# Second feed-forward block of a fused attention kernel: the hi/lo split of a pair of middle blocks is issued behind the next pair's Relu and sums, and the second product begins with six of eight pairs

## The chip, the cores and the metric

One core of a Trainium2 chip runs the whole program. The metric is the time of one execution on the device in microseconds (us), the median of several runs. Beside it there is one profiled execution, whose trace gives the start and the length of nearly every instruction on the core's engines: TensorE (PE; its weight loads are listed as PEld), VectorE (DVE), ScalarE (ACT), GpSimd (POOL) and SyncE (SP), which issues most DMAs.

## The reference

The input passes through causal-by-blocks attention (4 batches, 8 heads, 576 positions, 64 wide), a feed-forward block with layer norm, and a second feed-forward block behind a two-dimensional Fourier transform. All is float32. The change lies in the last two lines of the second block:

```python
def _moe2_ref(x, w_ch1, w_ch2):            # x: (4, 576, 512)
    X = np.fft.fft(x, axis=1)
    X = np.fft.fft(X, axis=2)
    mixed = np.real(X).astype(np.float32)
    u = x + mixed
    mu = np.mean(u, axis=-1, keepdims=True)
    var = np.mean((u - mu) ** 2, axis=-1, keepdims=True)
    un = (u - mu) / np.sqrt(var + 1e-06)
    ch = np.maximum(un @ w_ch1, 0.0) @ w_ch2   # 512 -> 2048 -> 512
    return (u + ch).astype(np.float32)
```

## The kernel before

**Tiles and chunks.** The 2304 tokens are handled in nine chunks of 256, named E0 to E3, F0 to F3 and L; a chunk's rows lie in a tile X as two halves of 128 tokens. float32 products are made of float16 ones: each operand is split into a high and a low half, hi = float16(x) and lo = float16(x - hi), and three of the four products hi x hi, hi x lo and lo x hi are added up in PSUM. So each block of a product is three matmuls.

**The second feed-forward block.** E0 and F0 go through it in the plain way. The other seven chunks, in the order E1, F1, E2, F2, E3, F3, L, use a Strassen-like scheme (seven block products in place of eight) for the second product, and the change is in these.

- *First product* (`s_gemm1`, called for i = 0 to 7). Unit i makes two blocks of the middle layer, i and i + 8 ("a pair"), each from 12 matmuls with 256 columns, into one PSUM bank `g`. Five such banks go round. The weights are tiles `wq`, the layer-normed tokens the tile `xnT`, of which there is one.
- *Evacuation* (`s_out`, once for each pair). Two Relus on ScalarE (L693) write the four 128 x 128 sub-blocks of the pair into a float32 tile `hr` (four of them go round). Four sums and differences on VectorE (L701) add the Strassen combinations, so that there are seven operands of 128 x 128. ScalarE then copies all seven to float16, the hi half (L702), and VectorE subtracts to get the lo half (L703), both into a tile `hs`; one `hs` tile holds two pairs, so a chunk has hs0, hs2, hs4 and hs6.
- *Second product* (`s_gemm2_steps`, eight steps). Step function `mm(p, hb, nm, i0, i1)` adds up, in the PSUM tile `s` of product p, operand hb of pairs i0 to i1 - 1 against the prepared weights T[nm] (names beginning with tB or tT): three matmuls a pair, 24 for a whole product, 168 for the seven. Three banks go round for `s`. `got(p)` adds a finished product into X on VectorE (L726, L732, with one copy to `su` on ScalarE, L738), and `put` sends a half of X to the output.
- *Layer norm of the next chunk* stands between these steps in four parts (`ln_steps`): VectorE normalizes into `xn` (L563), ScalarE makes the hi half in `xs` (L571), VectorE the lo half (L577), and a DMA on SP's queue transposes `xs` into `xnT` (L578). There is one `xs` and one `xnT`, so each half waits for the transpose before it, and the first transpose waits until the first product of the present chunk has read `xnT`.

**What sets the order.** `ffn_items` lists the work of the chunks, the first product's eight units and then the second product's eight steps, and `merge` interleaves it with other streams by the weights that stand beside each item (2.62 for a unit; 2.3, 2.3, 0.6 and 2.6 for the steps). The framework then puts each engine's instructions in order by the place in the program less a priority: `prio(f, n)` moves what f issues ahead by n places. `s_out` has S7P = 20. Each engine runs its own list in order; engines wait for each other by semaphores.

Of the kernel before, what the change touches and what calls it, by code (L numbers as in the profile page):

```python
# [12 lines left out]
AF = mybir.ActivationFunctionType  # L13
ALU = mybir.AluOpType
# [66 lines left out]
RK = (3, 4, 0, 1, 2, 5, 5.5)  # L81
PLAIN2 = (("E", 0), ("F", 0))
YP = 60
S7P = 20
R_T = 1.0
BLOCKS = ("B11", "B21", "B22", "T1", "T3", "T2", "T4")

# [2 lines left out]
def fused_kernel(ctx: ExitStack, tc: tile.TileContext, io: dict):  # L90
    nc = tc.nc
# [13 lines left out]
    def g_tile(shape, name):  # L105


        pool = psg
        if "x" in psn:
            pool = psn["x"] if psn["n"] % (GB + GX) >= GB else psg  # L110
            psn["n"] += 1
        return pool.tile(shape, F32, tag="g", name=name)

    def d_tile(name):
        return psn["d"].tile([128, 512], F32, tag="s", name=name)
# [394 lines left out]
    def w1(ffn, k, hl, m):  # L510
        o = 512 * k + 128 * (m % 4)
        return W[ffn, 1, m // 4][:, hl, o:o + 128]
# [5 lines left out]
    hT = {}  # L518
# [151 lines left out]
    def s_gemm1(c, i):  # L670

        if i % 2 == 0:
            t = wpool.tile([128, 2, 2, 7, 128], F16, tag="w", bufs=9, name=f"hs{i}")
            hT[2, c] = hT.get((2, c), []) + [t]
        xt = xnT[2, c]
        ps = g_tile([128, 2, 256], "g1")
        for q in range(2):
            n = 0
            for k in range(KT):
                for wh, xh in ((0, 0), (0, 1), (1, 0)):  # L680
                    nc.tensor.matmul(  # L681
                        out=ps[:, q, :], lhsT=w1(2, k, wh, i + 8 * q), rhs=xt[:, xh, k, :],
                        start=(n == 0), stop=(n == 3 * KT - 1),
                    )
                    n += 1
        prio(s_out, S7P)(ps, hT[2, c][i // 2][:, i % 2], i // 4)

    def s_out(ps, h, j):

        r = fpool.tile([128, 8, 128], F32, tag="hT", bufs=4, name="hr")  # L690
        rf = r.rearrange("p b t -> p (b t)")
        for q in range(2):
            nc.scalar.activation(  # L693
                out=rf[:, 256 * q:256 * q + 256], in_=ps[:, q, :], func=AF.Relu,
                scale=W["tk"][:, j + 2 * q:j + 2 * q + 1],
            )
        for o, a, b, op in (
            (4, 0, 2, ALU.add), (6, 1, 0, ALU.subtract), (5, 4, 1, ALU.subtract),
            (7, 3, 5, ALU.subtract),
        ):  # L700
            nc.vector.tensor_tensor(out=r[:, o], in0=r[:, a], in1=r[:, b], op=op)  # L701
        nc.scalar.activation(out=h[:, 0], in_=r[:, 1:8], func=AF.Copy)  # L702
        nc.vector.tensor_tensor(out=h[:, 1], in0=r[:, 1:8], in1=h[:, 0], op=ALU.subtract)  # L703

    def s_gemm2_steps(c):

        st = {}
        x = X[c]

        inv = W["tk"][:, 6:7]  # L710

        def mm(p, hb, nm, i0=0, i1=8):
            if i0 == 0:
                st[p] = d_tile("s2")
            ps = st[p][:, 0:256]
            for i in range(i0, i1):
                h = hT[2, c][i // 2][:, i % 2]
                for hh, wh in ((0, 0), (0, 1), (1, 0)):
                    nc.tensor.matmul(  # L719
                        out=ps, lhsT=h[:, hh, hb], rhs=T[nm][:, wh, i],  # L720
                        start=(i == 0 and hh == 0 and wh == 0), stop=(i == 7 and hh == 1),
                    )

        def x_add(t, d, p=None):
            o = x[:, t, 256 * d:256 * d + 256]
            nc.vector.scalar_tensor_tensor(  # L726
                out=o, in0=st["u"] if p is None else st[p][:, 0:256], scalar=inv, in1=o,
                op0=ALU.mult, op1=ALU.add,
            )

        def u_add(p):
            nc.vector.tensor_tensor(out=st["u"], in0=st["u"], in1=st[p][:, 0:256], op=ALU.add)  # L732

        @(lambda f: prio(f, YP))
        def got(p):
            if p == 1:
                st["u"] = wpool.tile([128, 256], F32, tag="w", bufs=9, name="su")
                nc.scalar.activation(out=st["u"], in_=st[1][:, 0:256], func=AF.Copy)  # L738
                x_add(1, 0, 1)
            elif p == 2:  # L740
                x_add(1, 0, 2)
            elif p == 6:
                u_add(6)
                x_add(0, 0)
            elif p == 5:
                u_add(5)
                x_add(1, 1)
                x_add(0, 1)
            elif p == 7:
                x_add(0, 1, 7)  # L750
                x_add(0, 0, 7)
            elif p == 3:
                x_add(1, 1, 3)
            else:
                x_add(0, 0, 4)

        def put(t):
            nc.sync.dma_start(out=io["out"][slot_of[c] + t], in_=x[:, t, :])

        A11, A22, A12, S1, S2, S3, S4 = range(7)  # L760
        return [
            (2.3, lambda: mm(1, A11, "B11", 0, 7)),
            (2.3, lambda: mm(2, A12, "B21", 0, 7)),
            (0.6, lambda: (
                mm(1, A11, "B11", 7, 8), got(1), mm(2, A12, "B21", 7, 8), got(2),
            )),
            (2.6, lambda: (mm(6, S2, "T2"), got(6))),
            (2.6, lambda: (mm(5, S1, "T1"), got(5))),
            (2.6, lambda: (mm(7, S3, "T3"), got(7))),
            (2.6, lambda: (mm(3, S4, "B22"), got(3), put(1))),  # L770
            (2.6, lambda: (mm(4, A22, "T4"), got(4), put(0))),
        ]
# [5 lines left out]
    def prio(f, n=None):  # L778
        def g(*a):
            if (n or AP) <= 0:  # L780
                return f(*a)
            with tc.high_priority(n or AP):
                return f(*a)
        return g
# [638 lines left out]
    if True:  # L1423
# [40 lines left out]
        def ffn_items(ffn, order, both=(), mixed=None):  # L1464
            seq = []
            for n, c in enumerate(order):
                x = ("X", ffn, c) if ffn == 2 else ("X1", c)
                lns = [(0.0, f, (x,), None) for _, f in ln_steps(ffn, c)]
                g1_needs = ()
                if ffn == 1 and n < LNA:  # L1470
                    LN.extend(
                        (w, prio(f, LNQ), need, ("LN", c) if i == 3 else None)
                        for i, (w, f, need, _) in enumerate(lns)
                    )
                    lns = []
                    g1_needs = (("LN", c),)
                g1 = [
                    (2.62, lambda mp=mp, c=c: gemm1(ffn, c, mp), (("W", ffn, 1, mp // 2),) + g1_needs,
                     ("G1", ffn, c, mp)) for mp in range(8)
                ]  # L1480
                if ffn == 2 and c not in PLAIN2:
                    g1 = [(2.62, lambda i=i, c=c: s_gemm1(c, i), (("W", 2, 1, 3),), None) for i in range(8)]
                    g2 = [
                        (w, lambda c=c, n=n: s_steps(c)[n][1](), (("W", 2, "T"),), None)
                        for n, w in enumerate((2.3, 2.3, 0.6, 2.6, 2.6, 2.6, 2.6, 2.6))
                    ]
                elif c in both or c == mixed:
                    g2 = [
                        (5.2, lambda q=q, c=c: gemm2_both(ffn, c, q), (("W", ffn, 2, q),),
                         ("F", ffn, c, q)) for q in range(4)  # L1490
                    ]
                else:
                    g2 = [
                        (2.59, lambda t=t, q=q, c=c: gemm2(ffn, c, t, q), (("W", ffn, 2, 3),),
                         ("F", ffn, c, q) if t == 1 else None) for t in range(2) for q in range(4)
                    ]
                if c == mixed:
                    g2 = sum(([g1[2 * q], g1[2 * q + 1], g2[q]] for q in range(4)), [])
                    g1 = []
                seq.append((lns, g1, g2))  # L1500
            out = []
            prev = []
            for n, (lns, g1, g2) in enumerate(seq):
                if ffn == 1 and n == 1:
                    out += lns + g1 + prev
                    prev = g2
                    continue
                k = len(prev) - 4
                out += prev[:k]
                for i in range(4):  # L1510
                    out += (prev[k + i:k + i + 1] if prev else []) + lns[i:i + 1]
                out += g1
                prev = g2
            return out + prev
# [150 lines left out]
```

## Time and profile before

| | before |
|---|---|
| median of 3 runs | 1037.1 us (1036.9 to 1037.69) |
| profiled execution, own time | 1038.49 us |
| its span, first to last instruction | 1036.6 us |
| mean granted clock of TensorE | 0.96 |
| PE busy | 930.3 us (90%) |
| PEld busy | 692.9 us (67%) |
| DVE busy | 739.8 us (71%) |
| ACT busy | 578.6 us (56%) |
| POOL busy | 82.8 us (8%) |

The span is what the trace shows; the execution's own time is what the runs are measured by, and it holds the span and the little around it. Matmuls are pipelined, so that one that is shown as 0.27 us long may follow the one before it after 0.11 us: the rate is read from the starts. The granted clock is 1.00 at TensorE's higher level and 0.50 at its lower one; a mean between them says how a stretch was divided.

### The profile page before, as it was taken

The numbers are of one execution on the slowest core, as the hardware profiler recorded it, in microseconds if no ns is written. First come the engines' busy times: TensorE is split into PE (matmuls) and PEld (weight loads), VectorE is DVE, ScalarE is ACT, GpSimd is POOL, SyncE is SP. The second block draws the span as 40 slices with busy tenths as digits, with TensorE's granted clock in tenths as the row PEclk, the third lists the DMA queues.
The fourth block names the chain that finished last, engine by engine and source line by source line (L and its number), as shares of the span: only waits on it lengthen the run. The fifth ranks groups of instructions, "written<-read, shape, count | busy, mean of one in ns | idle before, by whom it ended". The sixth has DMA issues, their size and how long they took to land.

```text
span 1036.6 us, 19852 instructions
## 1 busy us (share of the span) xinstructions
PE 930.3 (90%) x7730; PEld 692.9 (67%) x7730; DVE 739.8 (71%) x1821; ACT 578.6 (56%) x1017; POOL 82.8 (8%) x217
## 2 busy tenths in 40 slices
PE   5576879998889989999998989999989999999997
PEld 4464744575565674768574847685867878778786
DVE  5799898676867776675488988959856565464543
ACT  5698865777676776546366765526425243252331
POOL 2100101002002010040011011100000000000000
PEclk9688989999999999999998989999999999999999
DMA  7895834667648577454134467612010110101100
GB/s 219 233 265 146 246 74 128 127 126 158 139 100 170 116 148 131 83 175 163 21 117 115 135 187 272 228 62 71 15 39 12 31 22 22 41 12 32 22 21 22
DMA packets 173022, 115.13 MB, mean 111 GB/s; under 512 B 146957, under 2 KB 155158, under 8 KB 170880
## 3 DMA queue, kind: packets, MB, share of 16 engines
q1 hardware_dynamic: 170608, 109.60, 40.9%
q0 software_dynamic: 2320, 4.25, 1.6%
q8 instruction: 61, 1.00, 0.4%
q14 instruction: 33, 0.27, 0.1%
HBM read 64.15 MB, written 11.01 MB: 73 GB/s over the span
## 4 chain that ended last, share of the span: by engine, by line
PE 28%; DVE 20%; ACT 7%; DMA 2%; issue 2%; POOL 0%; ACTq 0%; DVEq 0%; POOLq 0%
PE s L719 11%; PE g L610 6%; DVE hs L703 5%; ACT hs L702 5%; PE g L635 5%; DVE hr L701 5%; PE g L662 2%; DMA wr<-in_w 2%; PE g L681 2%; DVE tT L444 1%; DVE hT L620 1%; DVE wt L440 1%; DVE ws L220 1%; DVE ws L217 1%; ACT wr L238 1%
## 5 line engine op out<-in xcount | busy, mean ns | idle before, releaser
L610 PEld LDWEIGHTS <-wq 128*128 128x128 f16 x2112 | 206.1, 99 | 50.3 <-ACT wq L330 8.5
L635 PE MATMUL g<-wq,hT 128*128 128x512 f16 x768 | 185.9, 381 | 0.0
L719 PEld LDWEIGHTS <-hs 128*128 128x128 f16 x1176 | 117.8, 101 | 39.4 <-ACT hs L702 13.2
L681 PEld LDWEIGHTS <-wq 128*128 128x128 f16 x1344 | 131.5, 98 | 15.4
L851 PE MATMUL pv<-vh,PT 128*128 128x65 f16 (+1 forms) x800 | 104.7, 202 | 31.0 <-DMA PT<-P 27.0
L635 PEld LDWEIGHTS <-hT 128*128 128x128 f16 x768 | 74.4, 98 | 85.1 <-issue 7.1
L851 PEld LDWEIGHTS <-PT 128*128 128x128 f16 x1200 | 83.2, 100 | 55.3 <-DMA PT<-P 29.4
L703 DVE TENSOR_TENSOR hs<-hr,hs 128x896 f16<-128x896 f32 x56 | 61.1, 1092 | 57.8 <-ACT hs L702 57.8
L702 ACT ACTIVATE hs<-hr 128x896 f16<-128x896 f32 x56 | 53.2, 950 | 80.1 <-DVE hr L701 74.9
L1063 PE MATMUL st<-k,qz 128*128 128x512 f16 (+2 forms) x288 | 79.6, 330 | 15.9 <-ACT e L1085 15.9
L693 ACT ACTIVATE hr<-g,tk 128x256 f32<-128x256 f32 x112 | 46.1, 462 | 80.9 <-PE g L681 80.9
L1085 ACT ACTIVATE e<-st,aq,acf 128x384 f32<-128x384 f32 (+2 forms) x80 | 56.8, 741 | 58.9 <-DVE aq L1080 54.9
L876 DVE SCALAR_TENSOR_TENSOR P<-e,P 128x768 f16<-128x768 f32 (+2 forms) x64 | 61.9, 970 | 38.2 <-ACT P L875 38.0
L719 PE MATMUL s<-tB,hs 128*128 128x256 f16 x504 | 68.6, 296 | 17.6 <-ACT hs L702 11.1
L719 PE MATMUL s<-tT,hs 128*128 128x256 f16 x672 | 75.8, 273 | 0.0
L620 DVE SCALAR_TENSOR_TENSOR hT<-g,hT 128x512 f16<-128x512 f32 x88 | 59.8, 683 | 18.3 <-ACT hT L619 18.1
L701 DVE TENSOR_TENSOR hr<-hr 128x128 f32<-128x128 f32 x224 | 56.6, 287 | 18.6 <-ACT hr L693 15.8
L851 PE MATMUL pv<-vl,PT 128*128 128x64 f16 (+1 forms) x400 | 65.3, 202 | 0.9 <-DVE vl L864 0.8
L662 PE MATMUL g<-wq,hT 128*128 128x512 f16 x288 | 65.5, 385 | 0.3 <-DVE wq L338 0.3
L619 ACT ACTIVATE hT<-g 128x512 f16<-128x512 f32 x88 | 51.4, 588 | 24.2 <-PE g L610 23.8
L875 ACT ACTIVATE P<-e 128x768 f16<-128x768 f32 (+2 forms) x64 | 54.8, 862 | 5.3 <-DMA PT<-P 4.0
L200 ACT ACTIVATE ws<-wr 128x512 f32<-128x512 f32 (+1 forms) x48 | 39.4, 831 | 24.0 <-DMA wr<-in_w 21.1
(416 smaller groups left out, 1654.9 us busy)
## 6 DMA issues: line engine op xcount, KB each, us to landing
wr<-in_w SPq DMA_DIRECT2D x16, 1024.0 KB, 5.9
wr<-in_w SPq DMA_DIRECT2D x32, 512.0 KB, 3.9
rawv<-in_vt SPq DMA_DIRECT2D x16, 320.0 KB, 3.6
rawqk<-in_kt SPq DMA_DIRECT2D x16, 288.0 KB, 2.8
d<-ws SPq DMA_DIRECT2D x4, 1024.0 KB, 5.5
ws<-d SPq DMA_DIRECT2D x4, 1024.0 KB, 8.6
wt<-d SPq DMA_DIRECT2D x4, 1024.0 KB, 6.2
rawqk<-in_qt SPq DMA_DIRECT2D x32, 80.0 KB, 3.3
```

Of the source, the lines that this page charges most:

```text
L610: nc.tensor.matmul(out=ps[:, i, :], lhsT=w1(ffn, k, wh, m), rhs=xt[:, xh, k, :], start=(n == 0), stop=(n == 3 * KT - 1),)
L620: nc.vector.scalar_tensor_tensor(out=h[:, :, 1, :], in0=ps, scalar=0.0, in1=h[:, :, 0, :], op0=ALU.max, op1=ALU.subtract,)
L635: nc.tensor.matmul(out=ps, lhsT=h[f // 4][:, f % 4, hh, t * 128:(t + 1) * 128], rhs=w2(ffn, f, wh), start=(f == 0 and hh == 0 and wh == 0) ...
L662: nc.tensor.matmul(out=g2["b"][t], lhsT=h[f // 4][:, f % 4, hh, t * 128:(t + 1) * 128], rhs=w2(ffn, f, wh), start=(f == 0 and hh == 0 and ...
L681: nc.tensor.matmul(out=ps[:, q, :], lhsT=w1(2, k, wh, i + 8 * q), rhs=xt[:, xh, k, :], start=(n == 0), stop=(n == 3 * KT - 1),)
L701: nc.vector.tensor_tensor(out=r[:, o], in0=r[:, a], in1=r[:, b], op=op)
L702: nc.scalar.activation(out=h[:, 0], in_=r[:, 1:8], func=AF.Copy)
L703: nc.vector.tensor_tensor(out=h[:, 1], in0=r[:, 1:8], in1=h[:, 0], op=ALU.subtract)
L719: nc.tensor.matmul(out=ps, lhsT=h[:, hh, hb], rhs=T[nm][:, wh, i], start=(i == 0 and hh == 0 and wh == 0), stop=(i == 7 and hh == 1),)
L851: nc.tensor.matmul(out=out[..., 0:w], lhsT=l, rhs=v[..., 0:w], start=(n == 0), stop=(n == len(mm) - 1))
L876: nc.vector.scalar_tensor_tensor(out=P[:, 1, 0:n], in0=e, scalar=PSC, in1=P[:, 0, 0:n], op0=ALU.mult, op1=ALU.subtract)
L1063: nc.tensor.matmul(out=st[:, h, 0:n] if j < 4 else sf[:, o:o + n], lhsT=qz[:, a, q:q + 128], rhs=k[:, c, o:o + n], start=(i == 0), stop=(j ...
```

## The change

In `s_out`, the hi copy and the lo subtraction of a pair are no longer issued with it. They are kept as a function `finish` in `s_lo`, and the call for the next pair issues them, behind that pair's second Relu on ScalarE and behind its last sum on VectorE (`tc.issue_after` holds an instruction of the same engine behind the one that is named). With the eighth pair, its own two are issued as well. The priority S7P becomes 400. In the second product, the two first sums begin with pairs 0 to 5 in place of 0 to 6, and the third step does pair 6 and then pair 7 of both. The weights of these steps in `merge` change with it.

```diff
-S7P = 20
+S7P = 400
...
-        prio(s_out, S7P)(ps, hT[2, c][i // 2][:, i % 2], i // 4)
+        late_lo = s_lo.pop("f", None)
+        prio(s_out, S7P)(ps, hT[2, c][i // 2][:, i % 2], i // 4, late_lo)
+        if i == 7:
+            prio(s_lo.pop("f"), S7P)()
...
-            nc.scalar.activation(
+            got = nc.scalar.activation(
...
-            nc.vector.tensor_tensor(out=r[:, o], in0=r[:, a], in1=r[:, b], op=op)
-        nc.scalar.activation(out=h[:, 0], in_=r[:, 1:8], func=AF.Copy)
-        nc.vector.tensor_tensor(out=h[:, 1], in0=r[:, 1:8], in1=h[:, 0], op=ALU.subtract)
+            done = nc.vector.tensor_tensor(out=r[:, o], in0=r[:, a], in1=r[:, b], op=op)
+        if late_lo is not None:
+            with tc.issue_after(got.ins), tc.issue_after(done.ins):
+                late_lo()
+
+        def finish():
+            nc.scalar.activation(out=h[:, 0], in_=r[:, 1:8], func=AF.Copy)
+            nc.vector.tensor_tensor(out=h[:, 1], in0=r[:, 1:8], in1=h[:, 0], op=ALU.subtract)
+
+        s_lo["f"] = finish
...
-            (2.3, lambda: mm(1, A11, "B11", 0, 7)),
-            (2.3, lambda: mm(2, A12, "B21", 0, 7)),
-            (0.6, lambda: (
+            (2.0, lambda: mm(1, A11, "B11", 0, 6)),
+            (2.0, lambda: mm(2, A12, "B21", 0, 6)),
+            (1.3, lambda: (
+                mm(1, A11, "B11", 6, 7), mm(2, A12, "B21", 6, 7),
                 mm(1, A11, "B11", 7, 8), got(1), mm(2, A12, "B21", 7, 8), got(2),
             )),
```

On ScalarE, at the end of the first product of chunk F1 (pairs 5, 6 and 7; `hr` are the Relus' output, `hs` the split operands, `xs` the next chunk's layer norm), this stood before:

```order
L693 ACTIVATE hr<-g_9694,tk 128x256 x2
L702 ACTIVATE hs_9659<-hr 128x896
L693 ACTIVATE hr<-g_9729,tk 128x256 x2
L702 ACTIVATE hs_9728<-hr 128x896
L693 ACTIVATE hr<-g_9763,tk 128x256 x2
L702 ACTIVATE hs_9728<-hr 128x896
L571 ACTIVATE xs<-xn 128x512
```

And this stands there in the changed program:

```order
L698 ACTIVATE hr<-g_9692,tk 128x256 x2
L712 ACTIVATE hs_9657<-hr 128x896
L698 ACTIVATE hr<-g_9727,tk 128x256 x2
L712 ACTIVATE hs_9657<-hr 128x896
L698 ACTIVATE hr<-g_9761,tk 128x256 x2
L712 ACTIVATE hs_9726<-hr 128x896 x2
L571 ACTIVATE xs<-xn 128x512
```

The copy behind each pair of Relus is now that of the pair before (the tile whose number ends in 57 is hs4, pairs 4 and 5; the one in 26 is hs6), and behind the last Relus the copies of pairs 6 and 7 stand together.

On VectorE, at the same place, this stood before:

```order
L701 TENSOR_TENSOR hr<-hr 128x128 x4
L703 TENSOR_TENSOR hs_9659<-hr,hs_9659 128x896
L701 TENSOR_TENSOR hr<-hr 128x128 x4
L703 TENSOR_TENSOR hs_9728<-hr,hs_9728 128x896
L701 TENSOR_TENSOR hr<-hr 128x128 x4
L703 TENSOR_TENSOR hs_9728<-hr,hs_9728 128x896
L577 TENSOR_TENSOR xs<-xn,xs 128x512
```

And this stands there in the changed program:

```order
L706 TENSOR_TENSOR hr<-hr 128x128 x4
L713 TENSOR_TENSOR hs_9657<-hr,hs_9657 128x896
L706 TENSOR_TENSOR hr<-hr 128x128 x4
L713 TENSOR_TENSOR hs_9657<-hr,hs_9657 128x896
L706 TENSOR_TENSOR hr<-hr 128x128 x4
L713 TENSOR_TENSOR hs_9726<-hr,hs_9726 128x896 x2
L577 TENSOR_TENSOR xs<-xn,xs 128x512
```

The four sums of a pair now stand ahead of the subtraction of the pair before; at the chunk's start the sums of pairs 0 and 1 follow each other, and at its end two subtractions do.

## Rows read from the trace of the kernel before

**Rows 1.** Span and mean granted clock of the core.

```profile
core 0: 1036.6 us, clock 0.960
```

**Rows 2.** TensorE in order of time: start, length, operation, count, [idle before <- releaser].

```profile
728.78 21.12 PE L681 MATMUL g<-xnT2('E', 1)_8972,wq 128*128 128x256 f16 x192
...
774.57 21.12 PE L681 MATMUL g<-xnT2('F', 1)_9427,wq 128*128 128x256 f16 x192
795.53 2.13 PE L719 MATMUL s<-tB,hs 128*128 128x256 f16 x18
799.02 0.39 PE L719 MATMUL s<-tB,hs 128*128 128x256 f16 x2 [1.37 <-ACT hs L702]
800.15 4.90 PE L719 MATMUL s<-tB,hs 128*128 128x256 f16 x28 [0.73 <-DVE hs L703]
...
817.98 21.12 PE L681 MATMUL g<-xnT2('E', 2)_9925,wq 128*128 128x256 f16 x192
...
843.57 2.79 PE L719 MATMUL s<-tB,hs 128*128 128x256 f16 x24 [0.73 <-DVE hs L703]
846.66 0.61 PE L719 MATMUL s<-tB,hs 128*128 128x256 f16 x4 [0.30 <-DVE hs L703]
...
860.21 21.12 PE L681 MATMUL g<-xnT2('F', 2)_10423,wq 128*128 128x256 f16 x192
...
1030.06 2.78 PE L719 MATMUL s<-tT,hs 128*128 128x256 f16 x24
```

**Rows 3.** ScalarE, VectorE and SP's queue in chunk F1, in order of time.

```profile
777.39 0.84 ACT L693 ACTIVATE hr<-g,tk 128x256 f32<-128x256 f32 x2 [14.82 <-PE g L681]
777.90 1.31 DVE L701 TENSOR_TENSOR hr<-hr 128x128 f32<-128x128 f32 x4 [2.64 <-ACT hr L693]
779.30 0.95 ACT L702 ACTIVATE hs<-hr 128x896 f16<-128x896 f32 x1 [1.07 <-DVE hr L701]
...
795.77 9.29 SPq L578 DMA_TRANSPOSE xnT2('E', 2)_9925<-xs  x2
...
798.02 0.95 ACT L702 ACTIVATE hs<-hr 128x896 f16<-128x896 f32 x1 [1.42 <-DVE hr L701]
798.88 0.82 ACT L693 ACTIVATE hr<-g,tk 128x256 f32<-128x256 f32 x2
799.00 1.09 DVE L703 TENSOR_TENSOR hs<-hr,hs 128x896 f16<-128x896 f32 x1 [1.07 <-ACT hs L702]
...
800.01 1.02 DVE L701 TENSOR_TENSOR hr<-hr 128x128 f32<-128x128 f32 x4
...
801.12 0.95 ACT L702 ACTIVATE hs<-hr 128x896 f16<-128x896 f32 x1 [1.42 <-DVE hr L701]
...
802.10 1.09 DVE L703 TENSOR_TENSOR hs<-hr,hs 128x896 f16<-128x896 f32 x1 [1.07 <-ACT hs L702]
803.11 0.68 DVE L577 TENSOR_TENSOR xs<-xn,xs 128x512 f16<-128x512 f32 x1
...
805.17 1.07 DVE L726 SCALAR_TENSOR_TENSOR XxF<-s,tk,XxF 128x256 f32<-128x256 f32 x2 [0.80 <-ACT su L738]
806.97 0.63 ACT L571 ACTIVATE xs<-xn 128x512 f16<-128x512 f32 x1 [1.83 <-DMA xnT2('E', 2)_9925<-xs]
```

**Rows 4.** The same view in chunk E1: its first hi copy on ScalarE.

```profile
736.18 0.95 ACT L702 ACTIVATE hs<-hr 128x896 f16<-128x896 f32 x1 [3.73 <-DVE ln2('F', 2)_10404 L538]
```

**Rows 5.** TensorE's waits from 728 us on: waiter, releaser, sum, times, longest.

```profile
PE s L719 <- ACT hs L702: 11.1, 8, 1.7
PE s L719 <- DVE hs L703: 6.5, 10, 0.7
```

**Rows 6.** Busy time by stretch: engines' busy us (instructions), then PEclk, DMA share, GB/s.

```profile
420.00:540.00 120.00, 120.00 (x954) 85.41 (x953) 78.50 (x189) 59.00 (x110) 16.17 (x32) 1.00 0.42 116
...
800.15:817.90 17.75, 17.75 (x148) 15.29 (x149) 11.34 (x35) 2.48 (x4) 0.00 (x0) 0.90 0.12 31
...
843.57:860.20 16.63, 16.32 (x148) 14.40 (x149) 10.20 (x33) 2.48 (x4) 0.00 (x0) 1.00 0.17 33
```

More of the change, by code (lines that the diff above doesn't have):

```diff
@@ L685, in s_gemm1, with s_out @@
                     n += 1
-        prio(s_out, S7P)(ps, hT[2, c][i // 2][:, i % 2], i // 4)
-    def s_out(ps, h, j):
+        late_lo = s_lo.pop("f", None)
+        prio(s_out, S7P)(ps, hT[2, c][i // 2][:, i % 2], i // 4, late_lo)
+        if i == 7:
+            prio(s_lo.pop("f"), S7P)()
+    s_lo = {}
+    def s_out(ps, h, j, late_lo):
         r = fpool.tile([128, 8, 128], F32, tag="hT", bufs=4, name="hr")
@@ L1484, in ffn_items @@
                         (w, lambda c=c, n=n: s_steps(c)[n][1](), (("W", 2, "T"),), None)
-                        for n, w in enumerate((2.3, 2.3, 0.6, 2.6, 2.6, 2.6, 2.6, 2.6))
+                        for n, w in enumerate((2.0, 2.0, 1.3, 2.6, 2.6, 2.6, 2.6, 2.6))
                     ]
```

## The prediction

> **What bounds the kernel now.** I read four views in this order. First the span and the median of the runs: 1036.6 us from the first to the last instruction [rows 1], and 1038.49 us as that execution's own time, so 1.89 us lie around the span. The unprofiled runs have their median at 1037.1 us, 1.4 us below the profiled one; my sum is made against the profiled span and its difference is then taken from the median.
>
> Second, TensorE in order of time over the last third [rows 2]. Seven chunks (E1, F1, E2, F2, E3, F3, L) go through the changed code from 728.78 us on. Each has 192 matmuls of the first product (eight units of 24) and 168 of the second, all with 256 columns. The first product of F1 runs from 774.57 to 795.53 us: 20.96 us / 192 = 0.1092 us a matmul, 2.62 us a unit. The second product has the same rate where nothing is waited for: 124 matmuls from 846.66 to 860.21 us, 0.1093 each. So a chunk without a wait would take 360 x 0.1092 = 39.3 us. F1 takes 817.98 - 774.57 = 43.41 us and E2 takes 860.21 - 817.98 = 42.23 us. All seven run from 728.78 to the last group's 1030.06 + 24 x 0.1092 = 1032.68 us: 303.9 us, where 7 x 39.3 = 275.1 us would do. **28.8 us** are lost.
>
> Where they are lost is seen in F1 [rows 2]. After 18 matmuls of the second product (795.53 + 1.96 = 797.49) TensorE waits 1.53 us, does two at 799.02, waits again until 800.15, 0.91 us, and then needs 17.83 us for 148 matmuls that take 16.16 at the full rate: 1.67 us more. 1.53 + 0.91 + 1.67 = 4.11 us, the whole of 43.41 - 39.30. The last term is the clock: its mean is 0.90 between 800.15 and 817.90 us, so part of the stretch was granted the lower of its two levels, 1.2 instead of 2.4 GHz, after the idle time before it; E2's stretch from 843.57 on has 1.00 [rows 6]. E2 pays 0.47 us of waiting for pair 7 instead (24 matmuls from 843.57 end at 846.19, the next begins at 846.66). The waits are put down to the hi copy on ScalarE (11.1 us in all) and the lo subtraction on VectorE (6.5 us) [rows 5], 17.6 us together; the rest of the 28.8 is the clock and what the modelled ends of matmuls hide.
>
> Third, ScalarE and VectorE in F1 [rows 3], with G0 to G7 for the ends of the eight units (774.57 + 2.62 each; G7 = 795.53). The first pair shows the bare latencies: Relus from G0 + 0.20 (777.39) for 0.84 us, sums from 777.90 for 1.31 us (G0 + 2.02), hi copy at 779.30 (0.09 later). Later pairs are a loop through both engines: hi copy of pair 6 at 798.02, of pair 7 at 801.12, 3.10 us a pair. It closes as 0.95 (copy) + 0.03 + 1.01 (lo subtraction at 799.00 to the next sums at 800.01) + 1.02 (sums) + 0.09, because on VectorE the sums of a pair stand behind the subtraction of the pair before, and that waits for ScalarE's copy. TensorE gives a pair in 2.62 us, so the loop falls 0.48 us behind at each. The last subtraction ends at 803.19, G7 + 7.66.
>
> **The change part by part.** *The order of the split.* No instruction is added or taken away: eight pairs of Relus, eight times four sums, eight copies, eight subtractions per chunk, each with its old duration. On ScalarE the copy of pair i-1 now stands behind the Relus of pair i, on VectorE its subtraction behind the sums of pair i. No engine's next step then depends on the other's last one: a pair costs ScalarE 0.82 + 0.95 = 1.77 us and VectorE about 1.02 + 1.09 = 2.11 us, both under 2.62 us [rows 3], so TensorE sets the pace and the lag does not grow. With the bare latencies: Relus of pair i end at Gi + 1.04, its sums at Gi + 2.02; the copy of pair i-1 runs from Gi + 1.06 to Gi + 2.01; its subtraction from Gi + 2.04 to Gi + 3.13, that is 0.51 us after the next unit's end, where the next sums want VectorE only at + 0.71.
>
> The new wait is the copy's: it could go at G(i-1) + 2.11 and goes at Gi + 1.06, 1.57 us later, since the Relus ahead of it wait for TensorE's unit i. Behind it stand the subtraction of the same pair and the Relus of pair i+1, which come 0.8 us after the copy's end. Nothing else is behind it until the eighth pair. At the end the order is Relus 7, copy 6, copy 7; sums 7, subtraction 6, subtraction 7: subtraction 6 ends at G7 + 3.13, copy 7 at + 3.06, subtraction 7 at about + 4.2 (before: G7 + 7.66).
>
> *Six of eight pairs.* The second product now does 18 matmuls on pairs 0 to 5 of the first sum and 18 on those of the second: 36 x 0.1092 = 3.93 us that need nothing newer than pair 5, whose subtraction ends at G6 + 3.13 = G7 + 0.51. Pair 6 is wanted at G7 + 3.93 (its lo two matmuls later, + 4.15), pair 7 at + 4.58 (lo + 4.80). Against + 3.13 and + 4.2, with about 0.1 us for the hop to TensorE, 0.9 and 0.5 us are left. So no wait remains, and without idle time I expect no lower clock: the clock was at 1.00 for 120 us from 420 to 540 us with TensorE busy throughout [rows 6].
>
> *What could come late next.* The layer norm of the following chunk stands behind copy 7 and subtraction 7. Its second half needs the tile xs, held by a DMA transpose that is queued on SP and goes out when the first product is through (795.77, G7 + 0.24). A subtraction into xs at 803.11 (0.68 us) let the next use of xs begin at 806.97 [rows 3], 3.2 us from its end, so the first transpose frees xs at about G7 + 3.2, just when copy 7 ends, and the second one lands at about G7 + 8.1 to 8.5. The next first product begins at G7 + 18.3: 10 us of cover. The first sum's evacuation (additions of 1.07 us at 805.17) would end at about G7 + 6.6; its PSUM bank is wanted by the fourth group at G7 + 18.3 - 4 x 2.62 = + 7.9. Both cost nothing, and without cover every us of lateness would be one per chunk.
>
> *E1.* It begins late: VectorE still builds weight sums and a layer norm, and its first copy starts at 736.18 [rows 4], against G0 + 2.11 = 733.51, 2.7 us late. At 2.1 us a pair against 2.62 it gains 0.5 us a pair back and is even after five or six of the seven that follow. I take nothing for it; if it gained nothing, 2.7 us less the 0.5 in hand would stay, 2.2 us once.
>
> **Sum.** 7 x 39.3 in place of 303.9: -28.8 us. Span 1036.6 - 28.8 = 1007.8; profiled time 1009.7; median 1037.1 - 28.8 = **1008.3 us**. That is also nearly the bound from below, since nothing ahead of 728 us and nothing behind the last matmul is touched.
>
> **The rivals.** *Small waits remain.* My margins of 0.5 to 0.9 us come from one chunk's rows. If the hops of the new order cost 1 us more, TensorE would wait 0.5 us per chunk: 3.5 us, 1012. Against it: the latencies I use are those of a pair that found both engines idle.
> *Small waits remain and the clock still falls.* F1 lost 1.67 us to the lower level behind waits of 2.44 us, E2 nothing behind the same two waits, so a wait can cost more than itself. With 0.5 + 1.67 us in each of seven chunks: 15.2 us less gain, 1024. The Trainium skill has this as a rule: "TensorE: Matmul & The Clock Gate", section "A second HAM failure mode: psum-queue depth-cycling", says that frequent short idle times between groups of matmuls make the clock go back and forth between its levels and that throughput suffers; F1's 0.90 agrees, E2's 1.00 does not.
> *The split is not what is waited for in time*, because the copies are held longer than I think: if subtraction 7 still ended at G7 + 7.7, TensorE would wait the old 2.9 us or so and only the clock could change: 303.9 - 7 x 42.2 = 8.5 us at most, 1029 to 1037.
> *Slower: the queues go in lock step.* If in the new order every pair had to go through Relus, sums, copy and subtraction one after the other, a pair would take 0.84 + 1.31 + 0.95 + 1.09 = 4.2 us; subtraction 7 would end 7 x (4.2 - 2.62) = 11 us later than in my sum, TensorE would wait 10.5 us per chunk against 4.1 now, and the time would be 1037.1 + 7 x 6.4 = 1082. It decides from about 3.3 us a pair on, where 7 x (3.3 - 2.62) - 0.6 equals 4.1. Against it: in the new order each copy waits only for sums that were done a pair earlier.
>
> **How the numbers follow.** My forecast 0.80; small waits 0.08; with the clock 0.06; split too late 0.03; slower 0.03. A measurement of this kernel tells about 0.2%, 2 us, from no change. All but the last two cases are faster by far, so faster 0.95, same 0.02, slower 0.03. The range goes from 1006, as an unprofiled run may lose more to the clock than the profiled one did (E2's and F1's periods differ by 1.2 us), to 1016, half of the way to the third case; 0.12 are left out above.
>
> **What would show it.** After: seven chunks of about 39.3 us in TensorE's timeline, the second product's 168 matmuls in 18.3 us with no wait for hs; mean clock 1.00 from 728 us on; copies 2.62 us apart in place of 3.10; the last subtraction at about 4.2 us after the first product's end in place of 7.7. I am wrong if copies stand more than 2.7 us apart, if the wait moves to xs or xnT, or if the clock falls without an idle TensorE.

## The result, and the profile after

| | before | after |
|---|---|---|
| median | 1037.39 us (4 runs, 1036.9 to 1040.38) | 1011.16 us (4 runs, 1007.94 to 1014.2) |
| ratio, 95% interval | | 0.9741 (0.9704 to 0.9778) |
| profiled execution, own time | 1038.49 us | 1009.95 us |
| its span | 1036.6 us | 1008.2 us |
| mean granted clock | 0.96 | 0.966 |

The change makes the kernel 2.6% faster. The forecast for the profiled execution was a span of 1007.8 and a time of 1009.7 us; the median is 2.9 us above the forecast of 1008.3, and the first experiment shows where such a difference can come from.

TensorE in order of time in the changed kernel (start, length, operation, count, [idle before]), the rows that answer to [rows 2]:

```profile
729.14 21.12 PE L681 MATMUL g<-xnT2('E', 1)_8972,wq 128*128 128x256 f16 x192
...
768.44 21.12 PE L681 MATMUL g<-xnT2('F', 1)_9427,wq 128*128 128x256 f16 x192
789.40 5.40 PE L731 MATMUL s<-tB,hs 128*128 128x256 f16 x48
794.64 8.02 PE L731 MATMUL s<-tT,hs 128*128 128x256 f16 x72
...
807.74 21.12 PE L681 MATMUL g<-xnT2('E', 2)_9925,wq 128*128 128x256 f16 x192
...
964.94 21.12 PE L681 MATMUL g<-xnT2L,wq 128*128 128x256 f16 x192
...
1001.62 2.78 PE L731 MATMUL s<-tT,hs 128*128 128x256 f16 x24
```

No row of the second product, in any of the seven chunks, has an idle time in front of it. E1 takes 768.44 - 729.14 = 39.30 us, F1 39.30 too, and six chunks 964.94 - 729.14 = 235.8 us, 39.30 each. From 729.14 to 1001.62 + 2.62 = 1004.24 us the seven take 275.1 us where they took 303.9: 28.8 us less, the whole forecast gain.

The busy time by stretch over these seven chunks, first in the kernel before, then in the changed one (us; PE, PEld, DVE, ACT and POOL busy; granted clock, DMA share, GB/s):

```profile
728.80:1032.70 303.90, 286.31 (x2521) 249.13 (x2519) 173.91 (x445) 105.39 (x188) 0.00 (x0) 0.97 0.09 24
```

```profile
729.20:1004.20 275.00, 275.00 (x2521) 246.41 (x2519) 182.06 (x445) 106.29 (x188) 0.00 (x0) 1.00 0.10 26
```

The same 2521 matmuls (the seven chunks' 2520 and the last one before them); TensorE is busy throughout, and its clock is at the higher level throughout, 2.4 GHz, where it had a mean of 0.97.

ScalarE, VectorE and SP's queue in F1 of the changed kernel, which answer to [rows 3]; G7, the end of its first product, is 789.40 us:

```profile
786.98 0.84 ACT L698 ACTIVATE hr<-g,tk 128x256 f32<-128x256 f32 x2 [0.94 <-PE g L681]
787.49 1.31 DVE L706 TENSOR_TENSOR hr<-hr 128x128 f32<-128x128 f32 x4 [0.31 <-ACT hr L698]
787.71 0.95 ACT L712 ACTIVATE hs<-hr 128x896 f16<-128x896 f32 x1
788.71 1.08 DVE L713 TENSOR_TENSOR hs<-hr,hs 128x896 f16<-128x896 f32 x1
...
789.64 5.81 SPq L578 DMA_TRANSPOSE xnT2('E', 2)_9925<-xs  x2
...
790.33 0.95 ACT L712 ACTIVATE hs<-hr 128x896 f16<-128x896 f32 x1
791.34 2.25 DVE L713 TENSOR_TENSOR hs<-hr,hs 128x896 f16<-128x896 f32 x2
791.51 0.95 ACT L712 ACTIVATE hs<-hr 128x896 f16<-128x896 f32 x1 [0.23 <-DVE hr L706]
792.72 0.63 ACT L571 ACTIVATE xs<-xn 128x512 f16<-128x512 f32 x1 [0.25 <-DMA xnT2('E', 2)_9925<-xs]
...
797.36 0.63 ACT L571 ACTIVATE xs<-xn 128x512 f16<-128x512 f32 x1 [2.46 <-DMA xnT2('E', 2)_9925<-xs]
```

The copies of pairs 5 and 6 start at 787.71 and 790.33, 2.62 us apart in place of 3.10. Relus wait for TensorE (0.94 us a pair) and the sums for the Relus (0.31): both engines have room now, and TensorE sets the pace. The last subtraction ends at 791.34 + 2.25 = 793.59, G7 + 4.19 where it was G7 + 7.66.

### The profile page after: what moved, and what is told of

Same layout as the page of the kernel before. It is cut to its first block, busy times and chain, and to the rows that moved or that the text cites. A ratio compares the mean times of both kernels' runs of the same rounds, so it can differ in the third digit from the quotient of the medians.

```text
span 1008.2 us, 19853 instructions
## 1 busy us (share of the span) xinstructions
PE 920.9 (91%) x7730; PEld 690.4 (68%) x7730; DVE 748.4 (74%) x1821; ACT 580.2 (58%) x1017; POOL 82.8 (8%) x217
## 4 chain that ended last, share of the span: by engine, by line
PE 47%; DVE 6%; ACT 2%; DMA 2%; issue 1%; POOL 0%; ACTq 0%; DVEq 0%; POOLq 0%
PE g L681 15%; PE s L731 13%; PE g L610 7%; PE g L635 7%; PE g L662 3%; DMA wr<-in_w 2%; DVE hT L620 1%; PE pq L1375 1%; ACT wr L238 1%; PE ya L1344 1%; DVE ws L220 1%; DVE ws L217 1%; DVE wq L338 1%; PE pq L1365 1%; PE pf L1365 1%
## 5 line engine op out<-in xcount | busy, mean ns | idle before, releaser
L864 PE MATMUL pv<-vh,PT 128*128 128x65 f16 (+1 forms) x800 | 104.8, 202 | 28.7 <-DMA PT<-P 26.2
L731 PEld LDWEIGHTS <-hs 128*128 128x128 f16 x1176 | 115.1, 98 | 13.3
L706 DVE TENSOR_TENSOR hr<-hr 128x128 f32<-128x128 f32 x224 | 64.9, 292 | 42.5 <-ACT hr L698 35.1
L731 PE MATMUL s<-tB,hs 128*128 128x256 f16 x504 | 57.3, 273 | 0.0
L1092 DVE TENSOR_REDUCE aq<-st 128x2 f32<-128x768 f32 (+2 forms) x48 | 46.6, 973 | 7.9 <-PE st L1076 5.0
```

The costliest lines, as they stand in the source:

```text
L706: done = nc.vector.tensor_tensor(out=r[:, o], in0=r[:, a], in1=r[:, b], op=op)
L731: nc.tensor.matmul(out=ps, lhsT=h[:, hh, hb], rhs=T[nm][:, wh, i], start=(i == 0 and hh == 0 and wh == 0), stop=(i == 7 and hh == 1),)
L864: nc.tensor.matmul(out=out[..., 0:w], lhsT=l, rhs=v[..., 0:w], start=(n == 0), stop=(n == len(mm) - 1))
```

## The experiments

My theory: the loop through both queues was what made the split late, and with it went both the waits and the lower clock; beginning with six pairs pays only on top. Rivals: that the six pairs alone do it; that one of the two queues alone does it; that what counts is the load of one engine and not the order. S7P is not a rival: with 20 in place of 400 the changed program, and with 400 in place of 20 the one before, have the same operations in the same order on ScalarE, VectorE and TensorE. The "kernel before" that ran beside the first four had a median of 1040.29 us (23 runs), beside the last three 1040.51 (13 runs).

**1. The changed kernel once more.** No edit.

> The changed kernel once more, for the spread of its times (1008 to 1014 us in four runs) and for a second profile. If the spread comes from the part ahead of the changed code, the seven chunks again take 39.3 us each without a wait, and the start of chunk E1's first product differs from 729.1 us by as much as the span differs from 1008.2. If it comes from the changed code, some chunk is longer than 39.3 us.

Median 1013.1 us (1012.65 to 1013.49, 4 runs), ratio 0.973 (0.9707 to 0.9753). TensorE's first product of E1 and of F1:

```profile
731.84 21.12 PE L681 MATMUL g<-xnT2('E', 1)_8972,wq 128*128 128x256 f16 x192
...
771.14 21.12 PE L681 MATMUL g<-xnT2('F', 1)_9427,wq 128*128 128x256 f16 x192
```

The chunk again takes 39.30 us. E1 begins 2.70 us later than in the first profile, and the span, 1010.9, is 2.7 us longer. So the difference between these two executions comes from ahead of the changed code. In the profiles of the kernels here E1 begins anywhere from 728.78 to 734.12 us.

**2. The order alone.** The two first sums take seven pairs as before:

```diff
-            (2.0, lambda: mm(1, A11, "B11", 0, 6)),
-            (2.0, lambda: mm(2, A12, "B21", 0, 6)),
-            (1.3, lambda: (
-                mm(1, A11, "B11", 6, 7), mm(2, A12, "B21", 6, 7),
+            (2.3, lambda: mm(1, A11, "B11", 0, 7)),
+            (2.3, lambda: mm(2, A12, "B21", 0, 7)),
+            (0.6, lambda: (
```

> The new order of the split with the old second product (seven of eight pairs first). My theory: TensorE reaches pair 6 at 1.96 us behind the first product's end (G7), its copy ends at G7 + 2.0 and its subtraction at G7 + 3.13, so TensorE waits about 1.0 us for pair 6 in each chunk and not at all for pair 7: 7 us over the changed kernel, a span of 1015, at a full clock. Rival, that beginning with six pairs is what pays and the order adds little: about 1030. Rival, that the order alone does it: 1008.

Median 1016.87 us (5 runs), ratio 0.9763 (0.9735 to 0.979); span 1013.3. TensorE in F1:

```profile
770.76 21.12 PE L681 MATMUL g<-xnT2('F', 1)_9427,wq 128*128 128x256 f16 x192
791.72 2.78 PE L731 MATMUL s<-tB,hs 128*128 128x256 f16 x24
794.80 2.79 PE L731 MATMUL s<-tB,hs 128*128 128x256 f16 x24 [0.30 <-DVE hs L713]
...
810.53 21.12 PE L681 MATMUL g<-xnT2('E', 2)_9925,wq 128*128 128x256 f16 x192
```

The chunk takes 39.77 us, 0.47 more than in the changed kernel and 3.6 less than F1 before. The one wait is for pair 6's subtraction, as expected, but half as long: 24 matmuls go ahead of it and not 20 (18 on pairs 0 to 5 and two on the hi half of pair 6), since the framework puts four of the second sum there. So the order is worth 303.9 - 7 x 39.77 = 25.5 of the 28.8 us, and the six pairs 7 x 0.47 = 3.3 us on top of it.

**3. Six of eight pairs alone.** The reverse of that edit, in the kernel before, with its order of the split.

> The old order of the split with the new second product (six of eight pairs first). My theory: the copies still stand 3.10 us apart and the last subtraction still ends 7.7 us behind the first product, so TensorE waits 2.9 us in each chunk (5.6 in E1) wherever it begins: 23 us over the changed kernel, a span of 1031, and up to 1037 if the clock falls in the chunks as before. Rival, that beginning with six pairs is what pays: 1008 to 1015.

Median 1042.27 us (12 runs), ratio 1.0022 (1.0000 to 1.0043); span 1039.6: no gain. TensorE in F1:

```profile
773.92 21.12 PE L681 MATMUL g<-xnT2('F', 1)_9427,wq 128*128 128x256 f16 x192
794.88 4.31 PE L719 MATMUL s<-tB,hs 128*128 128x256 f16 x38
799.50 0.61 PE L719 MATMUL s<-tB,hs 128*128 128x256 f16 x4 [0.31 <-DVE hs L703]
801.47 0.39 PE L719 MATMUL s<-tB,hs 128*128 128x256 f16 x2 [1.36 <-ACT hs L702]
802.60 0.92 PE L719 MATMUL s<-tB,hs 128*128 128x256 f16 x4 [0.73 <-DVE hs L703]
...
817.81 21.12 PE L681 MATMUL g<-xnT2('E', 2)_9925,wq 128*128 128x256 f16 x192
```

The stretch behind the last wait in F1, then in E3 (columns as in [rows 6]; the granted clock is the third figure from the end):

```profile
802.60:817.80 15.20, 15.20 (x124) 12.93 (x125) 9.26 (x30) 1.01 (x2) 0.00 (x0) 0.89 0.14 35
934.30:947.80 13.50, 13.50 (x124) 12.11 (x125) 6.50 (x14) 1.01 (x2) 0.00 (x0) 1.00 0.16 40
```

The 38 matmuls without a wait are there, and the waits have only moved from pair 6 to pair 7, which is no earlier. F1 takes 43.89 us. E3, at the higher clock, takes 947.84 - 905.61 = 42.23, just what E2 took before [rows 2]; in that stretch F1, E2, F2 and F3 have a mean clock of 0.89, and L has 0.88. The rival falls. The upper end of what I expected, 1037, was passed for two reasons. A lower clock behind the last wait costs more than it did before, 43.89 - 42.23 = 1.66 us a chunk in place of 43.41 - 42.23 = 1.18. And E2, which kept the higher level before, has the lower one here too.

**4. VectorE's load.** The subtraction of each pair is done twice, on the same values:

```diff
             nc.vector.tensor_tensor(out=h[:, 1], in0=r[:, 1:8], in1=h[:, 0], op=ALU.subtract)
+            nc.vector.tensor_tensor(out=h[:, 1], in0=r[:, 1:8], in1=h[:, 0], op=ALU.subtract)
```

> The changed kernel with the lo subtraction of every pair done twice (the second writes the same values). My theory: VectorE then needs 1.02 + 1.01 + 1.09 = 3.1 us a pair, over TensorE's 2.62, and sets the pace: the last subtraction ends 8.4 us behind the first product in place of 4.2, TensorE waits 3.7 us a chunk, 26 us in all or more with a lower clock: 1034 to 1045, no better than the kernel before. Rival, that the new order has room to spare and only the queueing mattered: under 1015.

Median 1038.82 us (12 runs), ratio 0.9977 (0.9958 to 0.9996): the gain is gone. The first products of F1 and E2, then VectorE in F1, whose first product ends at 800.62:

```profile
779.66 21.12 PE L681 MATMUL g<-xnT2('F', 1)_9435,wq 128*128 128x256 f16 x192
821.88 21.12 PE L681 MATMUL g<-xnT2('E', 2)_9941,wq 128*128 128x256 f16 x192
...
802.15 1.08 DVE L713 TENSOR_TENSOR hs<-hr,hs 128x896 f16<-128x896 f32 x1
803.27 1.09 DVE L714 TENSOR_TENSOR hs<-hr,hs 128x896 f16<-128x896 f32 x1
804.28 1.02 DVE L706 TENSOR_TENSOR hr<-hr 128x128 f32<-128x128 f32 x4
805.22 2.25 DVE L713 TENSOR_TENSOR hs<-hr,hs 128x896 f16<-128x896 f32 x2
807.38 2.09 DVE L714 TENSOR_TENSOR hs<-hr,hs 128x896 f16<-128x896 f32 x2
```

There is no idle time between VectorE's rows: it is the bound, with 805.22 - 802.15 = 3.07 us a pair, and is done at 809.47, G7 + 8.85. F1 takes 821.88 - 779.66 = 42.22 us where 39.3 is the pace of TensorE, so 2.9 us are lost and not the 3.7 expected. By 2.62 - 2.11 the new order has 0.5 us of room a pair, and this one microsecond more is past it.

**5. ScalarE's load.** The hi copy of each pair is done twice, in the same way.

> The changed kernel with the hi copy of every pair done twice (the second writes the same values). My theory: ScalarE then needs 0.84 + 0.86 + 0.95 = 2.65 us a pair, just at TensorE's 2.62, so hardly any lag grows, but at the end four copies stand in a row and the last subtraction ends about 5.9 us behind the first product, where TensorE wants it at 4.8: about 1.1 us of waiting a chunk, 8 us over the changed kernel, with chunks of 40.4 us. Rival, that only VectorE's load counts: chunks of 39.3 us, no loss.

Median 1020.35 us (4 runs), ratio 0.9807 (0.9772 to 0.9843). F1 takes 812.80 - 772.69 = 40.11 us, 0.81 over the changed kernel. The first products of F1 and E2, then ScalarE in F1, whose first product ends at 793.65:

```profile
772.69 21.12 PE L681 MATMUL g<-xnT2('F', 1)_9435,wq 128*128 128x256 f16 x192
812.80 21.12 PE L681 MATMUL g<-xnT2('E', 2)_9941,wq 128*128 128x256 f16 x192
...
796.41 0.93 ACT L712 ACTIVATE hs<-hr 128x896 f16<-128x896 f32 x1
797.25 0.61 ACT L571 ACTIVATE xs<-xn 128x512 f16<-128x512 f32 x1
797.77 0.93 ACT L713 ACTIVATE hs<-hr 128x896 f16<-128x896 f32 x1
```

ScalarE keeps the pace, as expected (its Relus start 2.62 us apart), and the loss is at the end of the chunk: the next chunk's layer norm (L571) stands between the two copies of pair 7, the second ends at 798.70 and the last subtraction 1.5 us later, G7 + 6.5 (5.9 was expected). That is 2.3 us later than in the changed kernel and costs only 0.81. The changed kernel's margin covers part of the difference (0.55 us, read in experiment 7). For the rest, the framework has put the hi products of pair 7 together and seven matmuls of the next product ahead of the two that need its lo half, nine matmuls or 0.98 us.

**6. The new order on ScalarE's queue alone.** The copy of a pair behind the next pair's Relus, its subtraction ahead of the next pair's sums:

```diff
+        sub = None
+        if late_lo is not None:
+            with tc.issue_after(got.ins):
+                sub = late_lo()
+        with ExitStack() as hold:
+            if sub is not None:
+                hold.enter_context(tc.issue_after(sub.ins))
...
                 done = nc.vector.tensor_tensor(out=r[:, o], in0=r[:, a], in1=r[:, b], op=op)
-        if late_lo is not None:
-            with tc.issue_after(got.ins), tc.issue_after(done.ins):
-                late_lo()
```

> The changed kernel with the new order on ScalarE's queue alone: the copy of a pair behind the next pair's Relus, but its subtraction ahead of the next pair's sums, as before the change. My theory: the loop through both engines is then closed again (subtraction, sums, copy: 3.1 us a pair) and starts 1.6 us later, since the first copy waits for the second pair's Relus; the last subtraction ends about 9.1 us behind the first product, TensorE waits 4.4 us a chunk: 1039 or, with a lower clock, up to 1050, slower than the kernel before. Rival, that it is ScalarE's order that opens the loop: 1008 to 1015.

Median 1039.83 us (10 runs), ratio 0.9998 (0.9972 to 1.0025): no gain. The first products of F1 and E2, then ScalarE and VectorE in F1, whose first product ends at 794.35:

```profile
773.39 21.12 PE L681 MATMUL g<-xnT2('F', 1)_9427,wq 128*128 128x256 f16 x192
816.24 21.12 PE L681 MATMUL g<-xnT2('E', 2)_9925,wq 128*128 128x256 f16 x192
...
791.94 0.95 ACT L716 ACTIVATE hs<-hr 128x896 f16<-128x896 f32 x1 [1.42 <-DVE hr L713]
...
792.92 1.09 DVE L717 TENSOR_TENSOR hs<-hr,hs 128x896 f16<-128x896 f32 x1 [1.07 <-ACT hs L716]
793.93 1.02 DVE L713 TENSOR_TENSOR hr<-hr 128x128 f32<-128x128 f32 x4
...
795.04 0.95 ACT L716 ACTIVATE hs<-hr 128x896 f16<-128x896 f32 x1 [1.42 <-DVE hr L713]
...
802.85 1.09 DVE L717 TENSOR_TENSOR hs<-hr,hs 128x896 f16<-128x896 f32 x1 [0.62 <-ACT hs L716]
```

The copies stand 3.10 us apart again, with the same two waits as before [rows 3]. The last subtraction ends at G7 + 9.6, later than before as forecast; the framework hides part of it by putting matmuls of the next product ahead, and F1 takes 816.24 - 773.39 = 42.85 us with its clock at 1.00. E2 and F2, with a mean clock of 0.96, take 44.22. I had expected it slower than the kernel before; by the interval it is the same.

**7. The new order on VectorE's queue alone.** Each copy at once, the subtraction behind the next pair's sums:

```diff
-            with tc.issue_after(got.ins), tc.issue_after(done.ins):
+            with tc.issue_after(done.ins):
                 late_lo()
+        nc.scalar.activation(out=h[:, 0], in_=r[:, 1:8], func=AF.Copy)
 
         def finish():
-            nc.scalar.activation(out=h[:, 0], in_=r[:, 1:8], func=AF.Copy)
             nc.vector.tensor_tensor(out=h[:, 1], in0=r[:, 1:8], in1=h[:, 0], op=ALU.subtract)
```

> The changed kernel with the new order on VectorE's queue alone: the subtraction of a pair behind the next pair's sums, but each copy behind its own pair's sums on ScalarE, as before the change. My theory: the sums no longer stand behind a subtraction that waits, and what is left is ScalarE's own chain of Relus, the wait for the sums and the copy, 2.8 us a pair: a lag of 0.2 us a pair, the last subtraction ends 5.6 us behind the first product and TensorE waits 0.9 us a chunk: chunks of 40.2 us, 6 us over the changed kernel. Rival, that both queues have to change: chunks of 42 us or more.

Median 1017.82 us (4 runs), ratio 0.9777 (0.9749 to 0.9805). The first products of E1, F1 and E2, then ScalarE and VectorE in F1, whose first product ends at 796.33:

```profile
733.05 21.12 PE L681 MATMUL g<-xnT2('E', 1)_8972,wq 128*128 128x256 f16 x192
775.37 21.12 PE L681 MATMUL g<-xnT2('F', 1)_9427,wq 128*128 128x256 f16 x192
815.00 21.12 PE L681 MATMUL g<-xnT2('E', 2)_9925,wq 128*128 128x256 f16 x192
...
793.83 0.95 ACT L710 ACTIVATE hs<-hr 128x896 f16<-128x896 f32 x1 [1.07 <-DVE hr L706]
...
796.40 1.08 DVE L713 TENSOR_TENSOR hs<-hr,hs 128x896 f16<-128x896 f32 x1
...
796.58 0.95 ACT L710 ACTIVATE hs<-hr 128x896 f16<-128x896 f32 x1 [1.07 <-DVE hr L706]
...
799.15 2.25 DVE L713 TENSOR_TENSOR hs<-hr,hs 128x896 f16<-128x896 f32 x2
```

Here the subtraction of one pair starts before the copy of the next; the loop through VectorE is open. What is left is ScalarE's own chain, 2.75 us a pair, and the last subtraction ends at 801.40, G7 + 5.07. F1 takes 815.00 - 775.37 = 39.63 us, 0.33 more than in the changed kernel (I had expected 0.9). The last subtraction is 5.07 - 4.19 = 0.88 us later than there and costs 0.33, so the changed kernel has 0.55 us to spare for pair 7; the prediction said 0.5. E1, whose split begins late, takes 775.37 - 733.05 = 42.32 us where the changed kernel takes 39.30: at 2.75 us a pair nothing of its lateness is made up. Together 3.0 + 6 x 0.33 = 5 us.

## Why the prediction was right

*What bounds it.* Right in place and size: chunks of 39.30 us against 39.3, a stage of 275.1 us against 275.1.

*The order of the split.* Right. The copies stand 2.62 us apart, subtractions end at G7 + 4.19 against "about + 4.2", and ScalarE and VectorE wait for TensorE. The experiments say more than the prediction did: it is the order on VectorE's queue, the sums ahead of a subtraction that waits, that opens the loop (experiment 7), and the copy's place behind the Relus alone gives nothing (experiment 6). The copy's place is worth 0.33 us a chunk and 3.0 us in E1, because without it ScalarE idles 1.07 us a pair for the sums, and the Relus of the next pair stand behind.

*The new wait of the copy* costs nothing, as said. By experiment 2 it would cost something without the six pairs: pair 6 is then late by 0.47 us.

*Six of eight pairs.* Right that no wait remains. Alone it gives nothing (experiment 3), since pair 7 ends the wait wherever it begins.

*What could come late next.* xs was free at 792.72, G7 + 3.3 (+ 3.2 was said), the second transpose done at 797.36, G7 + 8.0 (+ 8.1 to 8.5). No wait.

*E1.* Right that it catches up: 39.30 us like the others. But the 2.7 us of lateness were read against the old place of the first copy, G0 + 2.11. In the new order it is due at G1 + 1.06, which is 729.14 + 5.24 + 1.06 = 735.44 in the changed kernel. It starts at 736.54, 1.1 us late, and the fourth copy, at 743.23, is on time.

*The clock.* Right: 1.00 over the whole stage. How much of the 28.8 us was the clock's is only read from the rows before: F1 and E2 differ by 1.18 us, E2 at 1.00. F1, F2, F3 and L took 43.4 us each and E2 and E3 42.23, so about 4 x 1.18 = 4.7 us were the clock's, E1 left aside, and most of the rest was waiting.

*The rivals.* None of them came. The small waits need the split later than its margin allows, which experiment 5 made so, with 0.81 us a chunk. A split too late for the second product is what experiments 4 and 6 made (G7 + 8.9 and + 9.6), and there the time was that of the kernel before. Lock step, 4.2 us a pair, was seen in no run; the slowest were at 3.10.

*The median.* Forecast 1008.3, measured 1011.16. In the profile every term of the sum came out, so I put the difference down to the part ahead of the changed code: E1's start varies by up to 5 us between profiles of kernels with the same program ahead of it, and the three runs of before that I started from lay low in that spread (1036.9 to 1037.69; 23 more had a median of 1040.29). For the unprofiled runs this is argued and not shown, since they have no trace. From median to median the gain is 26.2 us, and 27.2 in experiment 1; both intervals hold 28.8 (23.0 to 30.7 us, and 25.7 to 30.5). What varies ahead of E1 stays open.

## What to carry to other kernels

When two engines hand work back and forth for each item of a loop, write down what stands behind what on each queue: the period is the length of the closed path through both queues, not the load of the busier one (here 3.10 us against 2.11 and 1.77). Issue the second engine's last step of an item behind its first step for the next item; that one move opened the path here, and moving the other engine's step alone did not. Reordering the consumer to begin with what is ready paid here only once the last item was early enough: 3.3 us behind the new order, nothing without it.

## What the runs showed of the hardware

The same waits do not always lower the clock: before, F1 and E2 waited alike up to the third piece of the second product, and only F1's next stretch was granted 0.90 [rows 6]. In experiment 6 likewise, of chunks with nearly the same waits F1, E3 and F3 had a mean clock of 1.00 and took 42.7 to 42.85 us, and E2 and F2 had 0.96 and took 44.22. With the subtraction doubled (experiment 4), the profile shows TensorE idle for 1.77 and 0.66 us in each chunk from E2 on, and from 821 to 1030 us the mean clock was 1.00:

```profile
821.00:1030.00 209.00, 196.85 (x1784) 173.09 (x1782) 155.31 (x321) 74.67 (x132) 0.00 (x0) 1.00 0.09 24
```

What decides between the two is not known from these runs. And a stretch at the lower level costs less where it lies over a wait: 1.18 us in F1 before, where pair 7 was late anyway, against 1.66 us behind the last wait in experiment 3.
